# q and k loaded in 32-token blocks and transposed on VectorE, in attention followed by a SoLU feed-forward

## The chip, the cores and the metric

The kernel runs on one core of a Trainium2 chip. The metric is the device time of one execution in microseconds (us). TensorE is called PE in the rows (PEld is its weight load), VectorE DVE, ScalarE ACT, GpSimd POOL; SP is the engine that issues most of the DMA transfers. Each engine works through its own queue of instructions in order, and a wait at the head of a queue holds everything behind it.

## The reference

```python
# q, k, v: (8, 12, 448, 64) float32; rmsnorm is over the 64 elements of a token's row
q_n, k_n = rmsnorm(q, g_q), rmsnorm(k, g_k)
scores = q_n @ k_n.transpose(0, 1, 3, 2) / sqrt(64)
attn = softmax(scores)                     # over keys
x = (attn @ v).transpose(0, 2, 1, 3).reshape(3584, 768)
h = x @ w_in                               # w_in: (768, 1024) float64
solu = h * softmax(h)
out = layernorm(solu) * g_ln @ w_out       # w_out: (1024, 768) float64
```

The weights arrive as 64-bit floats, which the kernel turns into 32-bit ones on the chip.

## The kernel before

The function `fast_path` does all the work; `general_path` is built beside it for large gains and isn't entered here.

**Attention** goes in 48 pairs of heads (8 batches of 6 pairs). In a pair, the 448 tokens lie on 112 partitions as 4 groups (`SP = 112`, `NJ = 4`), token `4p + j` on partition `p` of group `j`. `load` (L477) issues five DMAs on SP's queue: q and k of each head in pieces of 64 elements (256 bytes), and v in pieces of 1 KB. `norm` (L488) squares q and k on ACT (`sq`), sums each row on DVE (L494), and makes the inverse root with Ln and Exp on ACT and a correction step on DVE (L498 to L503). q is scaled by it on POOL (`qn`, L506); k is not scaled: its factor enters later as the scale of the Exp (L537). `qk_transpose` (L513) turns q and k with eight PE transposes of 112x112 into two PSUM tiles (`pt`), which DVE (with the gains, L524) and ACT (L522) copy to `qkT`. `scores` (L526) has four steps `kc`, one for each group of keys: two score matmuls (`s`), two Exps on ACT (`E`), and from the second step on a sum of the Exps on POOL (`es`, L541). `values` (L543) multiplies by v (`o`) and sums the Exps over the keys with a matmul by ones (`sm`), and DVE turns the sums into factors (`r`, `rc`) and writes the result `xT` (L568), at a stride of four elements.

**Weights**: `convert_w` (L450) converts one of 28 pieces: 12 of w_in, whose last product is on POOL (L465), and 16 of w_out, whose last product is on DVE (L468). The tile `tmp` carries it.

**Feed-forward** takes 28 tiles of 128 tokens: `ff_in` (`h`), `ff_solu` (`u`), `ff_transpose` (`pu`, `uT`) and `ff_out` (`po`, `y`).

**The order.** `pair` (L646) lists the pieces of pair n: the score steps, after step 0 the load of pair n+3, after step 1 the values of pair n-1, after step 2 the norm of pair n+2, after step 3 the transposes of pair n+1. Up to four feed-forward pieces go between them; the first may come from pair 12 on, and those of the second half from pair 24 on. The program's order is not the final one: a scheduler orders the instructions of each engine by when it thinks them ready. The buffers bind them too: q and k have 3 buffers, v has 4, `qkT` has 2, and the PSUM tiles `s`, `pt`, `o`, `sm`, `pu` and `po` share 6.

Of the kernel before, what the change touches and what calls it, by code (L numbers as in the profile page):

```python
# [366 lines left out]
def fast_path(  # L367
# [120 lines left out]
    def norm(n):  # L488
        d = st[n]
        sq = work.tile([SP, 2 * NJ * 2, D], FP32, tag="sq", name="sq", bufs=1)  # L490
        nc.scalar.activation(sq, d["qk"].rearrange("p s j h d -> p (s j h) d"), AF.Square)  # L491
        rs = d["rs"] = small.tile([SP, 2, NJ, 2], FP32, tag="rs", name="rs")
        flat = rs.rearrange("p s j h -> p (s j h)")
        nc.vector.tensor_reduce(flat, sq, AX, OP.add)  # L494

        x = small.tile([SP, 4 * NJ], FP32, tag="nx", name="nx")
        y = small.tile([SP, 4 * NJ], FP32, tag="ny", name="ny")
        nc.scalar.activation(y, flat, AF.Ln, scale=1.0 / D, bias=eps[0:SP])  # L498
        nc.vector.tensor_scalar(x, flat, -0.5 / D, -0.5e-6, OP.mult, OP.add)
# [291 lines left out]
```

## Time and profile before

| | |
|---|---|
| median of 3 runs | 1159.03 us (1157.96 to 1160.77) |
| profiled execution | 1159.19 us, of which the span from first to last instruction is 1157.4 us |
| PE busy | 1058.2 us (91% of the span) |
| DVE, ACT, POOL busy | 516.4, 410.9, 394.2 us |
| granted TensorE clock | 0.967 of full speed on average |
| DMA packets | 109047, of them 91056 under 512 bytes |

The shares are averages over stages with different limits. A stage is read from its own window: what is busy in it, at which clock, and which wait ends last. A row of the chain of waits names the work that ended last at each step; a row of a group gives the total busy time and the mean of one instruction in ns.

### The profile page before, as it was taken

The page shows a single profiled execution, that of the slowest core. Times are in us where ns is not written, and L with a number is a line of the kernel's source. Part 1 is how long each engine was busy: PE and PEld are TensorE (multiplying, and loading weights), DVE is VectorE, ACT ScalarE, POOL GpSimd, SP SyncE. Part 2 cuts the span into 40 slices and gives each one's busy share as a digit, 9 for nine tenths or more (in the row PEclk, how much of TensorE's full clock was granted, in tenths as well). Part 3 has the DMA queues.
Part 4 walks back from the last instruction along what each step waited for, and adds up shares of the span by engine and source line. Part 5 has one row for each costly group of instructions (what it writes and reads, how often), then busy time and mean ns, then how long its engine had stood idle before and what let it go on. Part 6 is the DMA issues. An engine that isn't in the chain of part 4 may idle for free.

```text
span 1157.4 us, 10878 instructions
## 1 busy us (share of the span) xinstructions
PE 1058.2 (91%) x3905; PEld 483.1 (42%) x3905; DVE 516.4 (45%) x922; ACT 410.9 (35%) x773; POOL 394.2 (34%) x242
## 2 busy tenths in 40 slices
PE   4666998998768999999999999999999999999997
PEld 2222333342223444444444444444444444455554
DVE  5897446678775333343432334333322333312300
ACT  4554664245555423333323233333322322111111
POOL 4766774245456323233222232232223232100000
PEclk8878999998898999999999999999999999999999
DMA  7421222113332111111111111111111000000001
GB/s 193 143 80 46 63 68 54 52 45 103 89 103 63 48 37 38 38 39 39 38 37 39 38 39 45 24 37 38 46 33 50 23 14 1 14 28 14 14 28 43
DMA packets 109047, 57.50 MB, mean 50 GB/s; under 512 B 91056, under 2 KB 101816, under 8 KB 108984
## 3 DMA queue, kind: packets, MB, share of 16 engines
q1 hardware_dynamic: 104640, 45.63, 15.3%
q10 hardware_dynamic: 4344, 11.08, 2.4%
q8 instruction: 33, 0.54, 0.2%
q14 instruction: 30, 0.25, 0.1%
HBM read 45.68 MB, written 11.01 MB: 49 GB/s over the span
## 4 chain that ended last, share of the span: by engine, by line
PE 73%; DVE 12%; ACT 6%; DMA 4%; issue 3%; POOL 1%; SPq 1%; ACTq 0%; POOLq 0%; DVEq 0%
PE po L630 26%; PE h L587 24%; PE s L533 10%; PE o L553 8%; ACT E L537 2%; PE sm L559 2%; DMA qk<-in_k_dram 2%; PE pt L520 2%; DMA raw<-in_moe_w_out_dram 1%; PE pu L620 1%; DVE tmp L456 1%; DVE rs L494 1%; DVE tmp L463 1%; SPq L485 1%; DVE xT L568 1%
## 5 line engine op out<-in xcount | busy, mean ns | idle before, releaser
L587 PE MATMUL h<-w_in,xT 128*128 128x512 f32 x672 | 310.8, 609 | 17.4 <-DVE xT L568 13.1
L537 ACT ACTIVATE E<-s,rs 112x448 f32<-112x448 f32 x384 | 222.3, 633 | 274.8 <-PE s L533 272.5
L630 PE MATMUL po<-w_out,uT 128*128 128x384 f32 x896 | 301.3, 491 | 5.7 <-ACT uT L621 5.1
L541 POOL TENSOR_TENSOR es<-es,E 112x896 f32<-112x896 f32 x96 | 205.3, 2138 | 257.1 <-ACT E L537 256.3
L533 PE MATMUL s<-qkT 64*112 64x448 f32 x768 | 194.6, 609 | 32.5 <-DVE qkT L524 27.8
L630 PEld LDWEIGHTS po<-w_out,uT 128*128 128x128 f32 x896 | 166.3, 190 | 134.4 <-ACT uT L621 13.2
L587 PEld LDWEIGHTS h<-w_in,xT 128*128 128x128 f32 x672 | 124.1, 193 | 171.6 <-issue 161.0
L541 POOL TENSOR_TENSOR es<-E 112x896 f32<-112x896 f32 x48 | 101.9, 2124 | 244.7 <-ACT E L537 244.4
L553 PE MATMUL o<-E,v 112*64 112x448 f32 x768 | 161.5, 561 | 0.0
L533 PEld LDWEIGHTS s<-qkT 64*112 64x112 f32 x768 | 63.1, 184 | 147.4 <-issue 113.1
L596 DVE TENSOR_REDUCE hmax<-h 128x1 f32<-128x1024 f32 x28 | 34.2, 1222 | 171.3 <-PE h L587 171.3
L631 ACT COPY y<-po 128x384 f32<-128x384 f32 x56 | 26.7, 477 | 225.1 <-PE po L630 225.1
L494 DVE TENSOR_REDUCE rs<-sq 112x16 f32<-112x1024 f32 x48 | 58.4, 1218 | 103.4 <-ACT sq L491 103.1
L553 PEld LDWEIGHTS o<-E,v 112*64 112x64 f32 x768 | 52.6, 141 | 107.6 <-issue 90.1
L563 DVE STREAM_TRANSPOSE r<-sm 128x448 f32<-128x448 f32 x48 | 30.9, 643 | 112.5 <-PE sm L559 112.5
L506 POOL TENSOR_TENSOR qn<-qk,rs 112x512 f32<-112x512 f32 x48 | 53.5, 1115 | 76.5 <-PE pt L520 58.6
L491 ACT ACTIVATE sq<-qk 112x1024 f32<-112x1024 f32 x48 | 50.7, 1057 | 80.5 <-DMA qk<-in_k_dram 80.3
L524 DVE TENSOR_SCALAR qkT<-pt,gcol 128x448 f32<-128x448 f32 x48 | 32.3, 673 | 104.7 <-PE pt L520 104.6
L520 PE MATMUL pt<-ident,qn 112*128 112x112 f32 x192 | 30.4, 284 | 34.0 <-DVE r L563 9.4
L610 POOL TENSOR_TENSOR he<-he,mhalf 128x1 f32<-128x1 f32 x28 | 15.6, 557 | 107.8 <-DVE he L609 107.4
L568 DVE TENSOR_TENSOR xT<-o,r 128x448 f32<-128x448 f32 x48 | 46.4, 970 | 4.9 <-PE h L587 3.7
L520 PEld LDWEIGHTS pt<-ident,qn 112*128 112x128 f32 x192 | 20.0, 147 | 65.2 <-DVE r L563 11.6
(54 smaller groups left out, 676.7 us busy)
## 6 DMA issues: line engine op xcount, KB each, us to landing
qk<-in_q_dram SPq DMA_DIRECT2D x96, 112.0 KB, 3.0
qk<-in_k_dram SPq DMA_DIRECT2D x96, 112.0 KB, 3.0
v<-in_v_dram SPq DMA_DIRECT2D x48, 224.0 KB, 2.7
out_dram<-y ACTq DMA_DIRECT2D x28, 384.0 KB, 2.3
raw<-in_moe_w_in_dram SPq DMA_DIRECT2D x12, 512.0 KB, 5.2
raw<-in_moe_w_out_dram SPq DMA_DIRECT2D x16, 384.0 KB, 3.4
grow<-in_g_q_dram ACTq DMA_DIRECT2D x2, 0.2 KB
grow<-in_g_k_dram ACTq DMA_DIRECT2D x2, 0.2 KB
```

The costliest lines, as they stand in the source:

```text
L491: nc.scalar.activation(sq, d["qk"].rearrange("p s j h d -> p (s j h) d"), AF.Square)
L494: nc.vector.tensor_reduce(flat, sq, AX, OP.add)
L506: nc.gpsimd.tensor_tensor(d["qn"], d["qk"][:, 0].rearrange("p j h d -> p (j h) d"), rs[:, 0].rearrange("p j h -> p (j h) ()").to_broadcast ...
L520: nc.tensor.transpose(pt[:, j * SP : (j + 1) * SP], src, ident[0:SP, 0:SP])
L533: nc.tensor.matmul(s, d["qkT"][hh, 1, kc * SP : (kc + 1) * SP], d["qkT"][hh, 0, :], start=True, stop=True)
L537: nc.scalar.activation(d["E"][:, kc, h], d["s", h], AF.Exp, scale=d["rs"][:, 1, kc, h : h + 1])
L541: nc.gpsimd.tensor_tensor(d["es"], d["E"][:, 0] if kc == 1 else d["es"], d["E"][:, kc], OP.add)
L553: nc.tensor.matmul(o[h * D : (h + 1) * D, :], d["v"][:, h, kc * D : (kc + 1) * D], d["E"][:, kc, h], start=(kc == 0), stop=(kc == NJ - 1),)
L568: nc.vector.tensor_tensor(xTs[b // 2][:, hp, c0 : c0 + S].rearrange("d (p j) -> d j p", j=NJ), o.rearrange("d (j p) -> d j p", j=NJ), r.re ...
L587: nc.tensor.matmul(d["h"][:, hs], xTs[m][:, c, i * P : (i + 1) * P], w_in[:, c, hs], start=(c == 0), stop=(c == KD - 1))
L596: nc.vector.tensor_reduce(nmax, d["h"], AX, OP.max, negate=True)
L630: nc.tensor.matmul(po, d["uT"][:, c], w_out[:, c, hs], start=(c == 0), stop=(c == KF - 1))
```

## The change

- q and k come in 32-token blocks: a partition holds one token of a block for one head and one half of the 64 elements (2 heads x 2 halves x 32 tokens = 128 partitions), and 14 blocks of 32 elements lie side by side. Each of the 8 DMAs writes 32 partitions in pieces of 128 bytes. v comes with token `112 j + p` on partition `p`, in pieces of 256 bytes.
- The squares and sums are over half rows (`part`). A product on PE with a constant matrix `fold` (`ss`, 28 columns) adds the two halves and puts the sum on both partitions. The inverse root is as before, on 28 columns.
- POOL now scales q and k (`qkn`, 128x896), and the Exp has no scale any more.
- One DVE transpose of 32x32 blocks (128x896) makes `qkT`, and ACT multiplies its q half by the gains. The eight PE transposes, `pt` and the two copies are gone.
- With the tokens in order, `xT` is written without a stride.

```diff
+        nc.gpsimd.memset(fold, 0.0)
+        for g in range(4):
+            gs = slice(g * 32, g * 32 + 32)
+            for x in range(2):
+                nc.gpsimd.tensor_copy(fold[gs, g // 2, x], ident[gs, gs])
...
-        d["qk"] = loads.tile([SP, 2, NJ, 2, D], FP32, tag="qk", name="qk", bufs=3)
-        d["v"] = loads.tile([SP, 2, NJ * D], FP32, tag="v", name="v", bufs=4)
+        d["qk"] = loads.tile([P, 2, NB, 32], FP32, tag="qk", name="qk", bufs=3)
+        d["v"] = loads.tile([SP, 2, NJ, D], FP32, tag="v", name="v", bufs=4)
         for s, src in enumerate((q, k)):
-            for h in range(2):
-                nc.sync.dma_start(d["qk"][:, s, :, h], src[b, h0 + h].rearrange("(p j) d -> p j d", j=NJ))
-        nc.sync.dma_start(d["v"], v[b, h0 : h0 + 2].rearrange("h (p j) d -> p h (j d)", j=NJ))
+            for g in range(4):
+                nc.sync.dma_start(
+                    d["qk"][g * 32 : g * 32 + 32, s],
+                    src[b, h0 + g // 2].rearrange("(b t) (x d) -> x t b d", t=32, x=2)[g % 2],
+                )
+        nc.sync.dma_start(d["v"], v[b, h0 : h0 + 2].rearrange("h (j p) d -> p h j d", j=NJ))
...
+        nc.scalar.activation(sq, blocks, AF.Square)
+        nc.vector.tensor_reduce(part, sq, AX, OP.add)
+        ss = ps_t.tile([P, 2 * NB], FP32, tag="t", name="ss")
+        nc.tensor.matmul(ss, fold.rearrange("p h x t -> p (h x t)"), part, start=True, stop=True)
...
+        d["qkn"] = work.tile([P, 2 * NB, 32], FP32, tag="qkn", name="qkn")
         nc.gpsimd.tensor_tensor(
-            d["qn"],
...
+            d["qkn"], blocks, y.rearrange("p b -> p b ()").to_broadcast([P, 2 * NB, 32]), OP.mult
         )
...
-        for s in range(2):
-            pt = ps_t.tile([P, S], FP32, tag="t", name="pt")
-            for j in range(NJ):
...
-                nc.tensor.transpose(pt[:, j * SP : (j + 1) * SP], src, ident[0:SP, 0:SP])
-            if s:
-                nc.scalar.copy(d["qkT"][:, 1], pt)
-            else:
-                nc.vector.tensor_scalar(d["qkT"][:, 0], pt, gcol[:, KF : KF + 1], None, OP.mult)
+        nc.vector.transpose(d["qkT"].rearrange("p s t -> p (s t)"), d["qkn"].rearrange("p b d -> p (b d)"))
+        nc.scalar.activation(d["qkT"][:, 0], d["qkT"][:, 0], AF.Copy, scale=gcol[:, KF : KF + 1])
...
-            nc.scalar.activation(d["E"][:, kc, h], d["s", h], AF.Exp, scale=d["rs"][:, 1, kc, h : h + 1])
+            nc.scalar.activation(d["E"][:, kc, h], d["s", h], AF.Exp)
...
+        nc.vector.tensor_tensor(xTs[b // 2][:, hp, c0 : c0 + S], o, r.rearrange("d b i -> d (b i)"), OP.mult)
```

The scheduler orders the new program anew. Three places show what it makes of it. A number in a name is the serial number of the tile in the program.

PE before, in a pair of the second half, from the third score step (`s_4348`) to the next pair's first (`s_4426`):

```order
L533 MATMUL s_4348<-qkT_4265 112x448
L533 MATMUL s_4350<-qkT_4265 112x448
L587 MATMUL h_4341<-w_in_94,xT_2729 128x512 x6
L533 MATMUL s_4392<-qkT_4265 112x448
L533 MATMUL s_4394<-qkT_4265 112x448
L520 MATMUL pt_4400<-ident_92,qn_4243 128x112 x4
L520 MATMUL pt_4406<-ident_92,qk_4022 128x112 x4
L620 MATMUL pu_4413<-ident_92,u_3711 128x128 x4
L620 MATMUL pu_4419<-ident_92,u_3711 128x128 x4
L533 MATMUL s_4426<-qkT_4399 112x448
```

PE now, the same stretch:

```order
L538 MATMUL s_4220<-qkT_4143 112x448
L538 MATMUL s_4222<-qkT_4143 112x448
L510 MATMUL ss_4231<-part_4228,fold_94 128x28
L586 MATMUL h_4213<-w_in_95,xT_2649 128x512 x6
L538 MATMUL s_4266<-qkT_4143 112x448
L538 MATMUL s_4268<-qkT_4143 112x448
L619 MATMUL pu_4277<-ident_92,u_3605 128x128 x4
L619 MATMUL pu_4283<-ident_92,u_3605 128x128 x4
L538 MATMUL s_4290<-qkT_4273 112x448
```

The two fours of transposes (`pt`) after the fourth score step are gone, and one small product (`ss`) stands after the third.

ACT now, in the same pair (`E_4157`), from its second score step to its third; `sq_4493` belongs to the norm whose product is `ss_4497`, two pairs further on:

```order
L542 ACTIVATE E_4157<-s_4186 112x448
L542 ACTIVATE E_4157<-s_4188 112x448
L507 ACTIVATE sq_4493<-qk_4296 128x896
L542 ACTIVATE E_4157<-s_4220 112x448
L542 ACTIVATE E_4157<-s_4222 112x448
L514 ACTIVATE ny_4234<-ss_4231,eps_100 128x28
L516 ACTIVATE ny_4234<-ny_4234 128x28
```

ACT before, at the start of a pair (`E_4289`); `sq_4494` belongs to the norm that the Ln below it (`ny_4499`) goes on with:

```order
L522 COPY qkT_4265<-pt_4272 128x448
L491 ACTIVATE sq_4494<-qk_4296 112x1024
L631 COPY y_4278<-po_4279 128x384
L537 ACTIVATE E_4289<-s_4290,rs_4100 112x448
L537 ACTIVATE E_4289<-s_4292,rs_4100 112x448
L498 ACTIVATE ny_4499<-rs_4496,eps_99 112x16
```

The square stood four instructions ahead of its own Ln; now it stands two pairs ahead of it.

DVE before, in the third pair, where the weights are converted (`tmp`); each `tmp` number is another piece:

```order
L463 SCALAR_TENSOR_TENSOR tmp_427<-raw_333,tmp_427 128x512
L456 TENSOR_SCALAR tmp_519<-raw_425 128x512
L457 TENSOR_SCALAR tmp_519<-raw_425 128x512
L456 TENSOR_SCALAR tmp_611<-raw_517 128x512
L457 TENSOR_SCALAR tmp_611<-raw_517 128x512
L461 SCALAR_TENSOR_TENSOR tmp_519<-raw_425,tmp_519 128x512
L462 TENSOR_SCALAR tmp_519<-tmp_519 128x512
L463 SCALAR_TENSOR_TENSOR tmp_519<-raw_425,tmp_519 128x512
L461 SCALAR_TENSOR_TENSOR tmp_611<-raw_517,tmp_611 128x512
L456 TENSOR_SCALAR tmp_703<-raw_609 128x512
L494 TENSOR_REDUCE rs_485<-sq_483 112x16
```

DVE now, there, from the values of one pair to the values of the next:

```order
L572 TENSOR_TENSOR xT_289<-o_378,r_390 128x448
L508 TENSOR_REDUCE part_404<-sq_403 128x28
L515 TENSOR_SCALAR nx_409<-ss_407 128x28
L517 TENSOR_TENSOR nx_409<-nx_409,ny_410 128x28
L518 TENSOR_TENSOR nx_409<-nx_409,ny_410 128x28
L464 TENSOR_SCALAR tmp_431<-raw_341 128x512
L519 SCALAR_TENSOR_TENSOR ny_410<-nx_409,ny_410 128x28
L465 TENSOR_SCALAR tmp_431<-raw_341 128x512
L469 SCALAR_TENSOR_TENSOR tmp_431<-raw_341,tmp_431 128x512
L470 TENSOR_SCALAR tmp_431<-tmp_431 128x512
L528 STREAM_TRANSPOSE qkT_514<-qkn_417 128x896
L471 SCALAR_TENSOR_TENSOR tmp_431<-raw_341,tmp_431 128x512
```

The conversions stood two and three in a row ahead of attention's work; now one stands in each pair, among it.

## Rows read from the trace of the kernel before

**Rows 1.** Windows: stretch, length, busy us of PE, PEld, DVE, ACT, POOL; clock, DMA, GB/s.

```profile
0.00:25.00 25.00, 8.66 (x33) 4.77 (x34) 12.37 (x27) 12.93 (x23) 8.56 (x15) 0.95 0.69 173
25.00:173.80 148.80, 115.46 (x508) 45.50 (x508) 104.71 (x178) 84.90 (x158) 104.86 (x58) 0.87 0.31 86
173.80:263.50 89.70, 81.40 (x276) 33.50 (x277) 60.40 (x109) 35.17 (x66) 32.46 (x22) 0.95 0.20 54
263.50:373.60 110.10, 83.86 (x368) 32.37 (x369) 82.83 (x146) 61.39 (x118) 61.72 (x33) 0.89 0.33 86
373.60:1004.00 630.40, 624.40 (x2270) 287.01 (x2270) 227.64 (x413) 198.33 (x374) 183.90 (x113) 1.00 0.13 35
```

**Rows 2.** Timeline of PE: a pair's first scores; start, busy, [idle before].

```profile
25.03 3.33 PE L533 MATMUL s<-qkT 64*112 64x448 f32 x8 [4.29 <-DVE qkT L524]
...
173.76 1.76 PE L533 MATMUL s<-qkT 64*112 64x448 f32 x8 [0.73 <-DVE qkT L524]
...
373.61 1.01 PE L533 MATMUL s<-qkT 64*112 64x448 f32 x4 [0.76 <-DVE qkT L524]
...
734.88 1.01 PE L533 MATMUL s<-qkT 64*112 64x448 f32 x4 [0.97 <-ACT qkT L522]
```

**Rows 3.** Chain of waits between 600 and 740 us: start, us, what.

```profile
650.23 0.94 PE s L533 x4
651.17 0.92 PE pt L520 x8
652.09 5.17 PE h L587 x12
...
667.63 0.75 PE sm L559 x4
668.39 1.02 PE pu L620 x8
```

**Rows 4.** Groups of instructions by form: DVE's work that the change removes or resizes.

```profile
L494 DVE TENSOR_REDUCE rs<-sq 112x16 f32<-112x1024 f32 x48 | 58.4, 1218 | 103.4 <-ACT sq L491 103.1
...
L568 DVE TENSOR_TENSOR xT<-o,r 128x448 f32<-128x448 f32 x48 | 46.4, 970 | 4.9 <-PE h L587 3.7
...
L524 DVE TENSOR_SCALAR qkT<-pt,gcol 128x448 f32<-128x448 f32 x48 | 32.3, 673 | 104.7 <-PE pt L520 104.6
...
L565 DVE STREAM_TRANSPOSE r<-rc 128x448 f32<-128x448 f32 x48 | 30.8, 641 | 0.8
```

**Rows 5.** The same view: ACT and POOL.

```profile
L537 ACT ACTIVATE E<-s,rs 112x448 f32<-112x448 f32 x384 | 222.3, 633 | 274.8 <-PE s L533 272.5 <-POOL es L541 2.1
L541 POOL TENSOR_TENSOR es<-es,E 112x896 f32<-112x896 f32 x96 | 205.3, 2138 | 257.1 <-ACT E L537 256.3 <-POOL w_in L465 0.4
...
L506 POOL TENSOR_TENSOR qn<-qk,rs 112x512 f32<-112x512 f32 x48 | 53.5, 1115 | 76.5 <-PE pt L520 58.6 <-DVE rs L503 17.3 <-DMA qk<-in_k_dram 0.6
L491 ACT ACTIVATE sq<-qk 112x1024 f32<-112x1024 f32 x48 | 50.7, 1057 | 80.5 <-DMA qk<-in_k_dram 80.3
```

**Rows 6.** Timeline of one norm in the PE-bound stretch.

```profile
709.11 1.22 DVE L494 TENSOR_REDUCE rs<-sq 112x16 f32<-112x1024 f32 x1
...
711.49 0.17 DVE L503 SCALAR_TENSOR_TENSOR rs<-nx,ny 112x16 f32<-112x16 f32 x1
```

**Rows 7.** One line's instructions: ns min/median/max of L485's issues on SP.

```profile
L485 SPq DMA_DIRECT2D qk<-in_k_dram x96: 612/621/1485, 2.2 to 894.7; - x96
```

**Rows 8.** DMA issues of the page: KB of one, median us to landing.

```profile
qk<-in_k_dram SPq DMA_DIRECT2D x96, 112.0 KB, 3.0
```

**Rows 9.** Windows again, over one load of q and k alone.

```profile
703.00:709.00 6.00, 6.00 (x22) 3.21 (x20) 3.41 (x9) 2.39 (x5) 5.23 (x4) 1.00 0.34 78
```

**Rows 10.** One line's instructions: ns min/median/max of a small DVE product.

```profile
L501 DVE TENSOR_TENSOR nx<-nx,ny x48: 103/176/1549, 9.9 to 903.9; 112x16 f32<-112x16 f32 x48
```

More of the change, by code (lines that the diff above doesn't have):

```diff
@@ L389, in fast_path @@
     SP = S // NJ
+    NB = S // 32
     NP = H // 2
@@ L396, in fast_path @@
     UB = LAG + 2
-    assert H * D == DM and 2 * D == P and NJ * SP == S and B % 2 == 0 and 2 * S % P == 0
+    assert H * D == DM and 2 * D == P and NJ * SP == S and S % 32 == 0 and B % 2 == 0 and 2 * S % P == 0
     consts = ctx.enter_context(tc.tile_pool(name="consts", bufs=1))
@@ L407, in fast_path @@
     ones = consts.tile([P, D], FP32, name="ones")
+    fold = consts.tile([P, 2, 2, 32], FP32, name="fold")
     w_in = consts.tile([P, KD, DFF], FP32, name="w_in")
@@ L486, in load @@
-        nc.sync.dma_start(d["v"], v[b, h0 : h0 + 2].rearrange("h (p j) d -> p h (j d)", j=NJ))
+            for g in range(4):
[4 more added lines that the diff above has]
+        nc.sync.dma_start(d["v"], v[b, h0 : h0 + 2].rearrange("h (j p) d -> p h j d", j=NJ))
     def norm(n):
         d = st[n]
-        sq = work.tile([SP, 2 * NJ * 2, D], FP32, tag="sq", name="sq", bufs=1)
@@ L491, in norm @@
[L491 to L499, printed above, removed]
+        blocks = d["qk"].rearrange("p s b d -> p (s b) d")
@@ new lines, in norm @@
+        sq = work.tile([P, 2 * NB, 32], FP32, tag="sq", name="sq", bufs=1)
+        part = small.tile([P, 2 * NB], FP32, tag="part", name="part")
+        nc.scalar.activation(sq, blocks, AF.Square)
+        nc.vector.tensor_reduce(part, sq, AX, OP.add)
+        ss = ps_t.tile([P, 2 * NB], FP32, tag="t", name="ss")
+        nc.tensor.matmul(ss, fold.rearrange("p h x t -> p (h x t)"), part, start=True, stop=True)
+        x = small.tile([P, 2 * NB], FP32, tag="nx", name="nx")
+        y = small.tile([P, 2 * NB], FP32, tag="ny", name="ny")
@@ L500, in norm @@
+        nc.scalar.activation(y, ss, AF.Ln, scale=1.0 / D, bias=eps)
+        nc.vector.tensor_scalar(x, ss, -0.5 / D, -0.5e-6, OP.mult, OP.add)
         nc.scalar.activation(y, y, AF.Exp, scale=-0.5)
@@ L502, in norm @@
         nc.vector.tensor_tensor(x, x, y, OP.mult)
-        nc.vector.scalar_tensor_tensor(flat, x, 1.5, y, OP.add, OP.mult)
-        d["qn"] = work.tile([SP, NJ * 2, D], FP32, tag="qn", name="qn")
+        nc.vector.scalar_tensor_tensor(y, x, 1.5, y, OP.add, OP.mult)
+        d["qkn"] = work.tile([P, 2 * NB, 32], FP32, tag="qkn", name="qkn")
         nc.gpsimd.tensor_tensor(
-            d["qn"],
-            d["qk"][:, 0].rearrange("p j h d -> p (j h) d"),
-            rs[:, 0].rearrange("p j h -> p (j h) ()").to_broadcast([SP, NJ * 2, D]),
-            OP.mult,
+            d["qkn"], blocks, y.rearrange("p b -> p b ()").to_broadcast([P, 2 * NB, 32]), OP.mult
         )
@@ L553, in values @@
                 nc.tensor.matmul(
-                    o[h * D : (h + 1) * D, :], d["v"][:, h, kc * D : (kc + 1) * D], d["E"][:, kc, h],
+                    o[h * D : (h + 1) * D, :], d["v"][:, h, kc], d["E"][:, kc, h],
                     start=(kc == 0), stop=(kc == NJ - 1),
```

7 lines of the change are left out of this document (removed).

## Prediction

> **What bounds the kernel now.** I read the table of windows first, because the 40 slices of the page show that PE is not equally busy everywhere. [rows 1] cuts the span where a new regime begins: the start; pairs 1 to 11 (I call it A: 148.8 us, 13.53 per pair); pairs 12 to 15 (B1: 89.7 us, in which feed-forward tiles fill PE); pairs 16 to 23 (B2: 110.1 us, 13.76 per pair); pairs 24 to 47 (C: 630.4 us). The feed-forward tiles after 1004 us hold nothing that the change touches.
>
> In C, PE is busy 624.40 of 630.4 us at full clock; DVE (227.64), ACT and POOL are under 40%. What PE doesn't have to do there is gained nearly in full; what the other engines do more costs nothing as long as it comes in time. All idle time of PE in C is 6.0 us; the largest single wait that I found is the 0.97 us of [rows 2], a pair's first score waiting for ACT's copy of `qkT`, four times, 3.9 us in sum.
>
> In A and B2 no engine is full: in A PE is busy 115.46 of 148.8, DVE 104.71, POOL 104.86, ACT 84.90 [rows 1]. The granted clock is 0.87 there, and [rows 2] shows what that mean hides: pair 1's eight score matmuls take 3.33 us and pair 12's 1.76 us, so that PE falls to its lower level (1.2 GHz) in part of A, after waiting (4.29 us ahead of pair 1). These stages are bound by a loop of waits from engine to engine.
>
> **The change in C.** Taken off PE: eight transposes a pair, one step of 0.92 us in the chain [rows 3]. Added: `ss`, a product with 28 columns. The trace has none of that size. The nearest row is `pu`: eight transposes of 128x128 in 1.02 us, 0.13 each [rows 3]. A product of one such step is the lower end, 0.13; four steps, 0.5, the upper. I take two steps, 0.26. So 24 x (0.92 - 0.26) = **-15.8**. The ends of `ss` give -19.0 to -10.1. The idle 6.0 us may go (to -21.8), but I leave them: the four long waits lie where ACT also has the SoLU's exponential, and with the transposes gone PE only comes earlier to the copy of `uT` behind it.
>
> Two covers make that price valid. First, the fold must not find PE waiting. In the new order of PE `ss` stands between score steps, with a feed-forward piece (5.2 us, [rows 3]) behind it, but the square that feeds it stands two pairs earlier on ACT, so it is long done. Uncovered, PE would stand still for two Exps, the square and the reduce: 1.27 + 0.92 + 1.07 + 0.2 = 3.5 us a pair [rows 4, 5], the square and the reduce scaled by 896/1024. Second, the load must land ahead of that early square, which ACT takes in order, with the Exps behind it. SP now issues eight DMAs of 0.62 us for q and k, then 3.0 us to landing [rows 7, 8]: 8.0 us from the product `qkn` that frees the buffer. Between them PE has two feed-forward pieces and some scores, over 10 us; so it is hidden, with 1 to 5 us to spare.
>
> The other parts lie beside PE in C. DVE per pair: the copy of `qkT` goes (-0.67), the reduce loses an eighth (-0.15), `xT` without its stride lies between 0.64 (a 128x448 transpose) and 0.97 (as now), I take 0.70 (-0.27); the new block transpose of 128x896 costs 1.11 to 1.28, by 0.641 for half of it [rows 4]. Together about +0.1. POOL: `qkn` has 896 elements a row where `qn` had 512 in 1.115 us; scaled that is 1.95, and the `es` product of 896 with two inputs, 2.14, is the upper end [rows 5]. So +0.84 to +1.02 a pair, on an engine that is idle two thirds of C. ACT trades the copy (0.43 to 0.54) for the gain step of the same size, and the square shrinks by an eighth.
>
> **The change in A, B1 and B2.** B1 is PE-bound (81.40 of 89.7): four pairs x 0.66 = **-2.6**.
>
> A and B2 need a new loop. In the new order of A, the square stands in its own pair behind the Exps of step 2, and `qkn` stands on POOL ahead of the last `es`. From one pair's `sm` to the next this is in series: scores 0.94, two Exps 1.27, square 0.92, reduce 1.07, fold 0.26, norm 1.33 (from the reduce's end at 710.33 to 711.66, [rows 6]), `qkn` 1.95, `es` 2.14, `sm` 0.75: 10.6 us, some 10.9 with handing over [rows 3 to 6]. POOL's own work sums to 9.5 now (104.86 / 11) and 10.4 with the longer product; DVE's stays near 9.6, PE's falls from 10.5 to 9.8 [rows 1]. So 10.9 is the floor of the new loop, and 13.53 the present length. The conversions are also spread, one in each pair, where two and three stood ahead of attention's work in DVE's old order; this takes away long waits, but puts five or six DVE instructions into every pair's chain. I take the middle between floor and present, 12.2 us in A. The start: pair 1's scores begin at 25.03 [rows 2]; in the new order they stand behind the fold of the third load. SP has 26 issues of 0.62 us up to that load's last piece, 16.1 us; then 3.0 to land, square 0.92, reduce 1.07, fold 0.26, pair 0's last score step at half clock 1.9, and a good 1 us of handing over: 24.5 (up to 28 if SP or DVE come late). Pair 12 then begins at 24.5 + 11 x 12.2 = 158.7 where it is 173.8: **-15.1**. B2 by the same rule, the middle of 10.9 and 13.76: 12.3, 8 x 1.43 = **-11.7** (the ends: 0 and -22.9).
>
> DMA: one load of q and k has 3584 pieces of 128 bytes where it had 1792 of 256. [rows 9]: a load's 1792 pieces take 0.34 of 16 engines for 6 us, 32.6 engine-us, 18.2 ns a piece. At the same price for a smaller piece the new load takes 65 engine-us, 4.1 us of all 16; v's 896 pieces add 1.0. In a loop of 12 us beside 2.2 us for weights (0.31 x 13.53 less 2.0) that is hidden. The Trainium skill's page "DMA: Bandwidth & Descriptors", section "Specifications", speaks against such pieces: below 512 bytes a transfer falls off the line rate and is read, modified and written. It gives no price; all pieces of q and k were already below that size, and whether 128 bytes cost more than 256 no row here shows (the third rival).
>
> GpSimd's longer product may hold up DVE. [rows 10]: a small DVE product of 0.176 us in the median took 1.549 once. The Trainium skill, "SBUF — State Buffer", section "Terms", says that VectorE and GpSimd share a port pair by a lock held for a whole instruction, the loser blocking fully. The trace agrees by that maximum, if it was such a case. If each of 19 early pairs lost the 0.84 us that the product grows, the sum would be 16 us higher, 1130.
>
> **Sum.** The profiled execution took 1159.19 us, of which 1157.4 are the span; the median of the runs, 1159.03, is the same within 0.02%. -15.1 - 2.6 - 11.7 - 15.8 = -45.2; 1159.2 - 45.2 = **1114.0 us**.
>
> **The rivals.**
> (a) *The early loops gain nothing*: the fold makes PE wait for DVE each pair where the transposes had waited, and the half clock stays. For it: A's waits are on DVE already. Only C and B1 count: 1159.2 - 18.4 = 1140.8.
> (b) *The early loops run at their own length*, 10.9: A then is 24.5 + 11 x 10.9 = 144.4 (-29.4), B2 -22.9, in all -70.7: 1088.5. Against it: POOL would be 95% busy.
> (c) *Small pieces cost double*, 36 ns: q and k take 8.2 us of all 16 engines, v up to 2.0, weights 2.2: 12.4 a pair, some 13 with waits. A: 24.5 + 143 = 167.5 (-6.3), B2 -6.1, in all -30.8: 1128.4.
> (d) *Slower*: the fold stands in PE's queue with the next scores behind it; if the reduce stands behind a DVE conversion, which in turn is held up beside GpSimd's longer products, PE idles, falls to its lower clock, and the pair's matmuls double. At 17 us a pair A takes +37.7 and B2 +25.9, less 18.4: 1204. It decides from 14.6 us a pair on: 11 x (14.6 - 13.53) + 8 x (14.6 - 13.76) = 18.5, what C and B1 gain. The same mechanism in C needs loads that land late, 3.5 us in each of 24 pairs: +84 less the 45.2, also slower. Against it: the order has the square two pairs ahead there.
> (e) *It cancels out*: loops of about 14.6 us, 1159.
>
> **How the numbers follow.** Forecast 0.46, (a) 0.20, (b) 0.11, (c) 0.07, (d) 0.13, (e) 0.03. The range takes in (b) with 8 us for the unknown start and the idle time of C, and (a) with 6 us for a fold of four steps: 1080 to 1147. It leaves out (d), (e) and little more. A measurement of this kernel tells about 0.2%, 2.3 us, from no change: faster 0.84 (forecast, a, b, c), same 0.03, slower 0.13.
>
> **What would show it.** In the profile after: no `pt`; `ss` at about 0.26 us a pair; DVE's block transpose at 1.1 to 1.3; `qkn` at 1.95 to 2.14. PE some 99% busy at full clock in C, with C's length at about 615 us. Pair 12 beginning at about 159 us, pair 24 at about 344. For (a): pair starts where they are now up to 16. For (b): POOL over 90% busy in A. For (c): ACT's square waiting on the DMA of q and k, and a DMA share in A of twice 0.31. For (d): a lower granted clock in A, `ss` or the scores behind it waiting on DVE's reduce, and in C `ss` with a wait of microseconds. The forecast is wrong if C gains under 10 us, or if A's pairs stay above 13.5.

## The result, and the profile after

The changed kernel takes 1133.62 us (median; 1130.65 to 1134.83) where the kernel before took 1158.88 beside it: a ratio of 0.9776, interval 0.9753 to 0.9799. That is 25 us of the 45 that were forecast, within the range.

The table cuts every profiled execution at the first score matmul of pairs 1, 12, 16, 24 and 47, as the prediction did (its A, B1, B2 and C; "rest" begins with pair 47). Times in us; the last two columns are the median of the runs and the ratio to the kernel before with its 95% interval.

| kernel | start | A, 1–11 | B1, 12–15 | B2, 16–23 | C, 24–46 | rest | median | ratio |
|---|---|---|---|---|---|---|---|---|
| before | 25.0 | 148.7 | 89.7 | 110.1 | 602.2 | 181.6 | 1158.9 | 1 |
| forecast | 24.5 | 134.2 | 87.1 | 98.4 | 587.0 | 181.0 | 1114.0 | 0.961 |
| **after** | 28.7 | 136.7 | 83.5 | 107.8 | 595.3 | 180.4 | 1133.6 | 0.978 (0.975–0.980) |
| e1, gain step on VectorE | 28.2 | 135.7 | 87.4 | 111.3 | 593.5 | 180.2 | 1139.4 | 0.983 (0.981–0.985) |
| e2, no sums of Exps | 31.0 | 130.0 | 81.7 | 88.3 | 592.9 | 179.8 | 1103.9 | 0.952 (0.950–0.954) |
| e3, no fold | 31.8 | 205.7 | 90.0 | 104.6 | 598.1 | 180.2 | 1213.9 | 1.047 (1.045–1.049) |
| e4, pieces of 256 B | 30.6 | 136.9 | 83.5 | 107.9 | 595.3 | 180.5 | 1135.9 | 0.979 (0.978–0.981) |
| e5, scaling on VectorE | 29.9 | 131.6 | 84.1 | 109.0 | 594.1 | 180.2 | 1131.1 | 0.976 (0.974–0.977) |
| e6, before + tokens in order | 24.0 | 146.2 | 89.2 | 108.6 | 602.2 | 181.9 | 1149.0 | 0.990 (0.988–0.992) |
| e7, before + k scaled | 27.2 | 151.8 | 88.9 | 113.9 | 599.7 | 181.5 | 1164.3 | 1.003 (1.002–1.005) |
| e8, fold twice | 32.3 | 138.1 | 85.0 | 109.5 | 597.3 | 180.4 | 1144.8 | 0.988 (0.986–0.990) |
| e9, last sum on TensorE | 30.4 | 140.1 | 86.0 | 109.2 | 592.5 | 180.4 | 1137.9 | 0.982 (0.980–0.983) |
| e10, k issued by ScalarE | 30.0 | 138.4 | 85.2 | 105.3 | 593.2 | 180.4 | 1133.7 | 0.978 (0.976–0.980) |
| e11, fold a pair later | 25.3 | 201.5 | 94.9 | 133.3 | 589.6 | 180.3 | 1226.9 | 1.058 (1.056–1.061) |
| e12, fold of a constant | 28.4 | 165.6 | 95.3 | 107.0 | 606.7 | 180.2 | 1185.3 | 1.022 (1.019–1.025) |

The windows of the profile after, cut at the same places (columns as in [rows 1]):

```profile
0.00:28.74 28.74, 8.42 (x24) 4.16 (x26) 9.04 (x25) 9.62 (x19) 9.99 (x23) 0.95 0.75 147
28.74:165.45 136.71, 110.03 (x439) 39.30 (x437) 114.26 (x163) 75.19 (x155) 103.51 (x55) 0.90 0.45 98
165.45:248.99 83.54, 78.89 (x257) 30.74 (x254) 67.89 (x116) 34.87 (x70) 35.03 (x21) 1.00 0.26 53
248.99:356.80 107.81, 88.79 (x331) 31.80 (x329) 88.18 (x141) 53.62 (x115) 68.16 (x33) 0.89 0.40 84
356.80:981.00 624.20, 613.99 (x2133) 276.60 (x2130) 267.12 (x435) 184.43 (x383) 202.04 (x115) 0.99 0.17 36
```

The length of A in the kernel before is the sum of two regimes, which the mean of 13.53 us a pair hides. Cut at the first scores of pair 5, before and after:

```profile
25.03:102.50 77.47, 49.84 (x184) 18.99 (x185) 69.52 (x103) 39.76 (x73) 55.24 (x30) 0.76 0.37 109
102.50:173.76 71.26, 65.58 (x324) 26.44 (x323) 35.15 (x76) 45.14 (x85) 49.55 (x29) 0.99 0.25 62
```

```profile
28.74:76.71 47.97, 38.26 (x160) 13.86 (x158) 39.90 (x57) 27.31 (x56) 36.70 (x20) 0.89 0.47 102
76.71:165.45 88.74, 71.77 (x283) 25.44 (x281) 74.36 (x107) 47.87 (x99) 66.81 (x36) 0.90 0.44 96
```

In the kernel before, all 12 pieces of w_in are converted in pairs 1 to 4, which take 19.4 us each; pairs 5 to 11 take 10.2 each. In the changed kernel one piece is converted in every pair from 1 to 12, and the pairs take 12.0 and 12.7 us each. So the first four pairs gained 29.5 us, and the other seven lost 17.5.

Against [rows 1] VectorE has become busier in every stage from pair 1 on: 114.3 us instead of 104.7 in A, in a shorter stage, and 88.2 instead of 82.8 in B2. The groups by form say why (columns as in [rows 4, 5]):

```profile
L542 ACT ACTIVATE E<-s 112x448 f32<-112x448 f32 x384 | 189.9, 544 | 268.6 <-PE s L538 268.2
L521 POOL TENSOR_TENSOR qkn<-qk,ny 128x896 f32<-128x896 f32 x48 | 83.8, 1746 | 50.9 <-DVE ny L519 31.2 <-DMA qk<-in_k_dram 14.1 <-ACT E L542 3.5
L528 DVE STREAM_TRANSPOSE qkT<-qkn 128x896 f32<-128x896 f32 x48 | 53.0, 1105 | 53.6 <-PE s L538 37.3 <-POOL qkn L521 16.3
L508 DVE TENSOR_REDUCE part<-sq 128x28 f32<-128x896 f32 x48 | 51.7, 1078 | 98.7 <-ACT sq L507 98.5
L507 ACT ACTIVATE sq<-qk 128x896 f32<-128x896 f32 x48 | 45.8, 954 | 3.0 <-DMA qk<-in_k_dram 2.8
L517 DVE TENSOR_TENSOR nx<-nx,ny 128x28 f32<-128x28 f32 x48 | 45.7, 952 | 3.8
L529 ACT ACTIVATE qkT<-qkT,gcol 128x448 f32<-128x448 f32 x48 | 32.3, 672 | 104.4 <-DVE qkT L528 104.4
L572 DVE TENSOR_TENSOR xT<-o,r 128x448 f32<-128x448 f32 x48 | 29.8, 622 | 5.1 <-PE h L586 3.7
L510 PE MATMUL ss<-part,fold 128*128 128x28 f32 x96 | 20.1, 291 | 45.1 <-DVE part L508 45.1
```

The block transpose (1.105 us), the reduce (1.078), `qkn` (1.746) and `xT` (0.622) cost about what was reckoned or less; the gain step on ScalarE (L529) costs 0.672, where 0.43 to 0.54 was reckoned. What stands out is L517, a product of 28 columns: 0.952 us each in the mean. Its counterpart before, L501, had 0.305:

```profile
L501 DVE TENSOR_TENSOR nx<-nx,ny 112x16 f32<-112x16 f32 x48 | 14.6, 305 | 13.6 <-ACT ny L500 13.4
```

In the PE-bound stage the chain of waits shows the fold and the new stall (start, us, what):

```profile
626.27 0.94 PE s L538 x4
627.21 0.34 PE ss L510 x2
627.54 5.25 PE po L629 x16
...
680.53 0.99 PE s L538 x4
681.52 0.53 ACT E L542
682.05 1.09 ACT u L598 x2
683.14 0.43 ACT E L542
683.58 0.18 ACT ny L514
683.75 0.48 ACT uT L620
684.24 0.04 issue
684.28 5.43 PE po L629 x16
```

The fold takes 0.34 us of the chain, against 0.92 for the transposes [rows 3]. The stall of [rows 2] has moved to `po`, which waits for ScalarE's copy of `uT`; TensorE's timeline has it twice in five pairs:

```profile
684.28 5.43 PE L629 MATMUL po<-w_out,uT 128*128 128x384 f32 x16 [0.63 <-ACT uT L620]
716.28 5.43 PE L629 MATMUL po<-w_out,uT 128*128 128x384 f32 x16 [0.67 <-ACT uT L620]
```

In A the waits are these (who waited for whom: us in total, times, longest):

```profile
PE ss L510 <- DVE part L508: 22.4, 10, 3.0
POOL w_in L473 <- DVE tmp L471: 20.2, 11, 2.0
ACT qkT L529 <- DVE qkT L528: 19.1, 6, 3.2
```

TensorE is idle for 26.7 of 136.7 us there, and 22.4 of them stand at the fold: ScalarE's square and VectorE's reduce come right ahead of it in the same pair.

### The profile page after: what moved, and what is told of

The parts are those of the page before. It is cut to its first block, busy times and chain, and to the rows that moved or that the text cites. A ratio compares the mean times of both kernels' runs of the same rounds, so it can differ in the third digit from the quotient of the medians.

```text
span 1132.5 us, 10579 instructions
## 1 busy us (share of the span) xinstructions
PE 1042.8 (92%) x3617; PEld 461.7 (41%) x3617; DVE 573.7 (51%) x922; ACT 375.9 (33%) x773; POOL 420.9 (37%) x251
## 4 chain that ended last, share of the span: by engine, by line
PE 78%; DVE 9%; ACT 6%; DMA 3%; POOL 1%; issue 1%; SPq 1%; ACTq 0%; POOLq 0%; DVEq 0%
PE po L629 26%; PE h L586 24%; PE s L538 12%; PE o L558 11%; PE sm L564 2%; ACT E L542 2%; DVE part L508 2%; DMA raw<-in_moe_w_out_dram 1%; PE pu L619 1%; PE ss L510 1%; ACT sq L507 1%; ACT u L598 1%; POOL es L546 1%; DVE tmp L470 1%; DVE tmp L469 1%
## 5 line engine op out<-in xcount | busy, mean ns | idle before, releaser
L586 PE MATMUL h<-w_in,xT 128*128 128x512 f32 x672 | 304.4, 602 | 7.8 <-DVE u L599 3.6
L542 ACT ACTIVATE E<-s 112x448 f32<-112x448 f32 x384 | 189.9, 544 | 268.6 <-PE s L538 268.2
L538 PE MATMUL s<-qkT 64*112 64x448 f32 x768 | 211.4, 625 | 14.4 <-DVE r L568 8.6
L521 POOL TENSOR_TENSOR qkn<-qk,ny 128x896 f32<-128x896 f32 x48 | 83.8, 1746 | 50.9 <-DVE ny L519 31.2
L508 DVE TENSOR_REDUCE part<-sq 128x28 f32<-128x896 f32 x48 | 51.7, 1078 | 98.7 <-ACT sq L507 98.5
L528 DVE STREAM_TRANSPOSE qkT<-qkn 128x896 f32<-128x896 f32 x48 | 53.0, 1105 | 53.6 <-PE s L538 37.3
L568 DVE STREAM_TRANSPOSE r<-sm 128x448 f32<-128x448 f32 x48 | 30.9, 644 | 84.1 <-PE sm L564 84.1
L529 ACT ACTIVATE qkT<-qkT,gcol 128x448 f32<-128x448 f32 x48 | 32.3, 672 | 104.4 <-DVE qkT L528 104.4
L510 PE MATMUL ss<-part,fold 128*128 128x28 f32 x96 | 20.1, 291 | 45.1 <-DVE part L508 45.1
L564 PE MATMUL sm<-es,ones 112*64 112x448 f32 x192 | 45.5, 544 | 3.6 <-POOL es L546 3.3
L517 DVE TENSOR_TENSOR nx<-nx,ny 128x28 f32<-128x28 f32 x48 | 45.7, 952 | 3.8
```

The costliest lines, as they stand in the source:

```text
L508: nc.vector.tensor_reduce(part, sq, AX, OP.add)
L517: nc.vector.tensor_tensor(x, x, y, OP.mult)
L521: nc.gpsimd.tensor_tensor(d["qkn"], blocks, y.rearrange("p b -> p b ()").to_broadcast([P, 2 * NB, 32]), OP.mult)
L528: nc.vector.transpose(d["qkT"].rearrange("p s t -> p (s t)"), d["qkn"].rearrange("p b d -> p (b d)"))
L538: nc.tensor.matmul(s, d["qkT"][hh, 1, kc * SP : (kc + 1) * SP], d["qkT"][hh, 0, :], start=True, stop=True)
L542: nc.scalar.activation(d["E"][:, kc, h], d["s", h], AF.Exp)
```

## The experiments

**The wait on ScalarE (e1).** ScalarE stands at the gain step until VectorE's transpose is done, with Exps behind it (the third line above).

```diff
-        nc.scalar.activation(d["qkT"][:, 0], d["qkT"][:, 0], AF.Copy, scale=gcol[:, KF : KF + 1])
+        nc.vector.tensor_scalar(d["qkT"][:, 0], d["qkT"][:, 0], gcol[:, KF : KF + 1], None, OP.mult)
```

> The gain step of qkT goes from ScalarE to VectorE, right behind the block transpose. Theory (ScalarE's queue): in the changed kernel ScalarE waits 19.1 us in pairs 1 to 11 and 21.9 us in pairs 16 to 23 for VectorE's block transpose, with Exps queued behind the gain step; with the step on VectorE these waits are gone and the early stages lose 15 to 35 us: 1100 to 1118 us in all. Rival (VectorE is full): VectorE is 84% and 82% busy there and gets 0.3 to 0.7 us more a pair; the early stages stay or lengthen: 1130 to 1145 us. In pairs 24 to 47 both expect at most 2 us of change.

1139.4 us, within the rival's range. A gains 1.0 us, B1 and B2 lose 3.9 and 3.5. The wait on ScalarE was not what holds the early stages. On VectorE the step takes 1.016 us in the mean (L529 of e1), where 0.3 to 0.7 was expected; that this is what B1 and B2 lose by is likely, not shown.

**GpSimd and VectorE (e2, e5, e9).** e2 leaves the sums of the Exps out, e5 moves the scaling, e9 moves the third sum of the early pairs.

```diff
e2
-            nc.gpsimd.tensor_tensor(d["es"], d["E"][:, 0] if kc == 1 else d["es"], d["E"][:, kc], OP.add)
...
-            nc.tensor.matmul(sm[h * D : (h + 1) * D, :], ones[0:SP, :], d["es"][:, h], start=True, stop=True)
+            nc.tensor.matmul(sm[h * D : (h + 1) * D, :], ones[0:SP, :], d["E"][:, 3, h], start=True, stop=True)
e5
-        nc.gpsimd.tensor_tensor(
+        nc.vector.tensor_tensor(
             d["qkn"], blocks, y.rearrange("p b -> p b ()").to_broadcast([P, 2 * NB, 32]), OP.mult
e9
-        if kc:
+        if kc and not (kc == 3 and n < LAST_ON_PE):
...
+            parts = [d["es"][:, h]] + ([d["E"][:, 3, h]] if n < LAST_ON_PE else [])
+            for i, x in enumerate(parts):
```

> The sums of the Exps on GpSimd are left out (the sums over keys take the last group of keys alone), so GpSimd has only the scaling of q and k and the weight products. Theory (VectorE's instructions are stretched beside GpSimd's): the first correction product falls from 0.95 us to 0.2, the steps of the weight conversion from 1.4 to 1.7 us to 0.3 to 0.6, and VectorE's busy time from 574 to under 510 us; pairs 1 to 11 and 16 to 23 fall to 10 to 11 us each, in all 1085 to 1100 us. Rival (VectorE's stretching is off the path): the stages lose only what the last sum costs in the chain, 0 to 1 us a pair: 1115 to 1134 us.

1103.9 us, between the two ranges. The first correction product, one line's instructions (ns min/median/max), after and in e2:

```profile
L517 DVE TENSOR_TENSOR nx<-nx,ny x48: 133/918/2002, 11.0 to 918.3; 128x28 f32<-128x28 f32 x48
```

```profile
L517 DVE TENSOR_TENSOR nx<-nx,ny x48: 131/188/190, 13.3 to 889.1; 128x28 f32<-128x28 f32 x48
```

So this small product is held up by GpSimd's sums: no instruction of the line takes over 0.190 us once the sums are gone. The trace after shows it one by one: all 30 of the 48 that take over 0.2 us begin while a sum runs on GpSimd, and end 0.04 to 0.05 us after it. The Trainium skill, "SBUF — State Buffer", section "Terms", names such a hold: a lock on a port pair that the two engines share, held for a whole instruction. The trace agrees: the longest hold, 2.0 us, is about one sum of 2.1 us. The stages followed less than expected: B2 got 19.5 us shorter, A only 6.7. And e2 takes out two things at once, the hold and the sums in the chain. Its window of B2:

```profile
242.70:330.98 88.28, 80.50 (x331) 30.03 (x329) 67.15 (x143) 53.68 (x117) 13.97 (x8) 0.97 0.50 103
```

> The scaling of q and k goes from GpSimd to VectorE. Theory (in pairs 16 to 23 VectorE is held up beside GpSimd's products, of which this one has grown): GpSimd's busy time falls by 84 us, VectorE's own work grows by 1.2 us a pair (twice the 0.62 us of the 128x448 product), its stretched instructions get shorter; pairs 16 to 23 gain about 1 us each, pairs 1 to 11 nothing: 1122 to 1130 us. Rival (VectorE's own work is the bound): 1.2 us more in each of 19 early pairs: 1150 to 1160 us.

1131.1 us, whose interval overlaps that of the change; both numbers missed, the theory's by 1 us. The stages came out against the theory: A gains 5.1 us and B2 loses 1.2. VectorE is busy 101.5 of its 109.0 us in B2:

```profile
245.63:354.63 109.00, 89.05 (x330) 33.40 (x328) 101.47 (x152) 51.77 (x114) 53.15 (x25) 0.89 0.40 83
```

> The changed kernel, in which pairs 0 to 23 leave the third sum of Exps on GpSimd out and TensorE adds the last group of keys in the sums over keys (four more products, 0.75 us a pair); the result is the same. Theory (the early pairs are held by VectorE's being held up beside GpSimd's sums, and by the last sum in the chain): GpSimd has 2.1 us less a pair; pairs 1 to 11 gain 0.5 to 1 us each, pairs 16 to 23 1 to 2 us, pairs 12 to 15 lose 0.75: 1112 to 1124 us. Rival (TensorE at its lower clock is the bound there): 0 to 1 us more a pair: 1133 to 1150 us.

1137.9 us: the rival's number. In A and B2 GpSimd and VectorE have both become less busy, and both stages are longer:

```profile
30.40:170.46 140.06, 115.61 (x483) 43.47 (x481) 95.81 (x162) 75.77 (x154) 79.20 (x44) 0.90 0.43 95
170.46:256.50 86.04, 82.04 (x273) 32.45 (x271) 64.01 (x117) 35.56 (x72) 28.04 (x18) 1.00 0.26 52
256.50:365.70 109.20, 90.73 (x352) 34.97 (x350) 80.05 (x141) 51.99 (x113) 47.83 (x25) 0.88 0.40 83
```

TensorE's wait at the fold stays (22.9 us in A of e9), and its busy time grows by 5.6 us in A, where the stage grows by 3.3, and by 1.9 in B2, where the stage grows by 1.4. So neither VectorE's nor GpSimd's occupation alone is the bound, and that in e2 it was the hold which made B2 short is not shown.

**The pieces (e4).**

```diff
-                    d["qk"][g * 32 : g * 32 + 32, s],
-                    src[b, h0 + g // 2].rearrange("(b t) (x d) -> x t b d", t=32, x=2)[g % 2],
+                    d["qk"][g * 32 : g * 32 + 32, s].rearrange("t (b x) d -> t b (x d)", x=2),
+                    src[b, h0 + g // 2].rearrange("(x b t) d -> x t b d", t=32, x=2)[g % 2],
```

> q and k are loaded in pieces of 256 bytes, half as many, with the same number of transfers and bytes (a token's two halves then lie side by side, so what is computed is another function of the same size). The order on every compute engine is the same. Theory (the pieces are hidden): the DMA share of pairs 1 to 11 falls from 0.45 towards 0.35, the time stays within 4 us of the changed kernel: 1130 to 1137 us. Rival (small pieces hold up the early loads): pairs 1 to 23 gain 0.5 to 1 us each: 1110 to 1122 us.

1135.9 us, within the theory's range, and every stage from pair 1 on within 0.2 us of the change. The queue rows of the page (packets, MB, share of 16 engines), after and in e4:

```profile
q1 hardware_dynamic: 225984, 45.64, 20.3%
```

```profile
q1 hardware_dynamic: 139968, 45.64, 17.0%
```

86,016 more pieces cost 3.3% of 16 engines over 1132.5 us, 598 us: some 7 ns for each piece more, where a piece of 256 bytes took 18.2 [rows 9]. So two pieces of 128 bytes cost some 25 ns together, 12.6 each, and the time doesn't follow them. The Trainium skill ("DMA: Bandwidth & Descriptors", section "Specifications") asks for at least 512 bytes for the line rate; both sizes lie below that, so no run here compares across it.

**Parts of the change alone (e6, e7).** Both edit the kernel before.

```diff
e6
...
-                nc.sync.dma_start(d["qk"][:, s, :, h], src[b, h0 + h].rearrange("(p j) d -> p j d", j=NJ))
-        nc.sync.dma_start(d["v"], v[b, h0 : h0 + 2].rearrange("h (p j) d -> p h (j d)", j=NJ))
+                nc.sync.dma_start(d["qk"][:, s, :, h], src[b, h0 + h].rearrange("(j p) d -> p j d", j=NJ))
+        nc.sync.dma_start(d["v"], v[b, h0 : h0 + 2].rearrange("h (j p) d -> p h j d", j=NJ))
...
-            xTs[b // 2][:, hp, c0 : c0 + S].rearrange("d (p j) -> d j p", j=NJ),
...
+        nc.vector.tensor_tensor(xTs[b // 2][:, hp, c0 : c0 + S], o, r.rearrange("d b i -> d (b i)"), OP.mult)
e7
+        kk = d["qk"][:, 1].rearrange("p j h d -> p (j h) d")
+        nc.gpsimd.tensor_tensor(
+            kk, kk, rs[:, 1].rearrange("p j h -> p (j h) ()").to_broadcast([SP, NJ * 2, D]), OP.mult
+        )
...
-            nc.scalar.activation(d["E"][:, kc, h], d["s", h], AF.Exp, scale=d["rs"][:, 1, kc, h : h + 1])
+            nc.scalar.activation(d["E"][:, kc, h], d["s", h], AF.Exp)
```

> The kernel before with one part of the change alone: tokens in order on the partitions (v in pieces of 256 bytes), so that xT is written without a stride; the transposes on TensorE stay. Theory (this part pays little): the xT product falls from 0.97 to 0.62 us, 0.35 us a pair on VectorE, of which only the early pairs see something: 1150 to 1159 us. Rival (it was this part that made pairs 12 to 15 faster by more than TensorE's saving): 3 to 4 us there and as much in pairs 16 to 23: 1145 to 1150 us.

1149.0 us, a ratio of 0.990: the rival's number, and two fifths of what the whole change brought. But its stages are not the rival's. Its runs lie between 1145.7 and 1154.0, and the profiled one, at the slow end, shows only 5.3 us of the gain (A 2.5, B2 1.5, the start 1.0, B1 0.5), so where the rest lies is not seen.

> The kernel before with one part of the change alone: k is scaled on GpSimd too (one more product of 512 elements a row, 1.1 us), and the Exp has no scale; transposes on TensorE stay. Theory (GpSimd's longer occupation costs the early pairs): 0.5 to 1 us in each of 19: 1168 to 1178 us. Rival (the Exp without a scale, which fell from 0.633 to 0.544 us in the changed kernel, pays for it: 0.7 us a pair on ScalarE): 1150 to 1160 us.

1164.3 us, 0.3% slower, between the two ranges. A and B2 lose 3.1 and 3.8 us: GpSimd's longer work costs 0.3 to 0.5 us a pair there, less than expected, and C gains 2.5.

**The fold (e8, e3).**

```diff
e8
+        nc.tensor.matmul(ss, fold.rearrange("p h x t -> p (h x t)"), part, start=True, stop=True)
e3
-        ss = ps_t.tile([P, 2 * NB], FP32, tag="t", name="ss")
-        nc.tensor.matmul(ss, fold.rearrange("p h x t -> p (h x t)"), part, start=True, stop=True)
+        ss = part
```

> The changed kernel with the fold made twice. Theory (in pairs 24 to 47 TensorE is the bound, and the fold costs its own time): pairs 24 to 47 take 0.15 to 0.34 us more each, 4 to 8 us, the early pairs 0 to 2 us: 1138 to 1144 us. Rival (the fold is hidden behind other waits): within 2 us of the changed kernel, 1132 to 1136.

1144.8 us, just above the theory's end. In the steady part five pairs take 131.5 us where they took 130.6: 0.18 us for the second fold. C grows by 2.0 us only, the three early stages by 1.4 to 1.7 each, and the start, which varies between versions, by 3.5.

> The product that adds the two halves of a row is left out: the norm goes on with VectorE's half sums. Theory (the fold costs its own time on TensorE, 0.34 us a pair, in the stage of pairs 24 to 47, and 22.4 us of waiting in pairs 1 to 11 that something else would take over): pairs 24 to 47 lose 8 us, the earlier ones 0 to 8: 1118 to 1126 us. Rival (the wait at the fold is what holds the early pairs): pairs 1 to 11 lose 15 to 20 us more: 1100 to 1110 us.

1213.9 us: both failed. Without the fold A takes 205.7 us. C as a whole does not get shorter, though its steady part does: five pairs take 129.5 us instead of 130.6, so that the fold is worth 0.2 us a pair there, as in e8; pair 24 takes 35.2 us instead of 28.2. The scheduler orders the program anew, and TensorE waits elsewhere in A:

```profile
PE s L537 <- ACT qkT L528: 86.5, 10, 10.0
```

The scores now wait for the gain step of their own pair. That made the wait at the fold the question: what if it is taken away with the rest in its place?

**The wait at the fold (e11, e12).** e11 cuts the norm in two and puts the fold behind the values of the next pair; e12 leaves it in place and feeds it a constant.

```diff
e11
...
             if kc == 2 and n + 2 < B * NP:
-                pieces.append(lambda: norm(n + 2))
+                pieces.append(lambda: half_sums(n + 2))
             if kc == 1 and n:
                 pieces.append(lambda: values(n - 1))
+            if kc == 1 and 1 < n + 1 < B * NP:
+                pieces.append(lambda: norm(n + 1))
e12
+        nc.gpsimd.memset(same, 32.0)
...
-        nc.tensor.matmul(ss, fold.rearrange("p h x t -> p (h x t)"), part, start=True, stop=True)
+        nc.tensor.matmul(ss, fold.rearrange("p h x t -> p (h x t)"), same, start=True, stop=True)
```

> The changed kernel with the norm cut in two: squares and half sums of pair n+2 stay behind score step 2 of pair n, the fold and what follows come one pair later, behind the values of the next pair's step 1, so that 3.9 us of other products stand on TensorE between. Theory (in pairs 1 to 11 the wait at the fold, 22.4 of TensorE's 26.7 idle us, is what keeps the early loop long, through the lower clock too): pairs 1 to 11 take 112 to 124 us instead of 136.7, pairs 16 to 23 lose their 4.7 us of that wait: 1108 to 1120 us. Rival (VectorE and GpSimd are late anyway, and the wait moves to the scores, for the block transpose of the next pair): pairs 1 to 11 stay over 130 us: 1126 to 1136 us.

1226.9 us. A pair's first scores in TensorE's timeline of e11:

```profile
101.64 3.33 PE L544 MATMUL s<-qkT 64*112 64x448 f32 x8 [9.67 <-ACT qkT L535]
...
118.51 3.33 PE L544 MATMUL s<-qkT 64*112 64x448 f32 x8 [5.53 <-ACT qkT L535]
```

> The changed kernel, in which the fold multiplies a constant instead of the half sums (squares and half sums are still made, and nothing uses them), so that TensorE never waits at it, while the fold keeps its place behind score step 2 and all that follows it (the scaling, the block transpose, the gain step) stays. Theory (the wait for the half sums, 22.4 us in pairs 1 to 11 and 4.7 us in pairs 16 to 23, with the lower clock that follows it, is what the early stages' gain went into): pairs 1 to 11 take 108 to 122 us instead of 136.7, pairs 16 to 23 some 3 to 8 us less: 1100 to 1116 us. Rival (that wait only stands ahead of the next one, for the chain over GpSimd and VectorE to the next scores): pairs 1 to 11 stay above 128 us: 1124 to 1136 us.

1185.3 us. Its windows of A and B1, and what TensorE waits for in A:

```profile
28.42:194.01 165.59, 104.91 (x428) 36.30 (x428) 108.47 (x163) 73.41 (x153) 99.94 (x54) 0.83 0.35 80
194.01:289.34 95.33, 89.43 (x262) 34.52 (x264) 61.52 (x111) 34.75 (x69) 32.68 (x20) 0.93 0.25 49
```

```profile
PE s L540 <- ACT qkT L531: 60.3, 11, 8.5
```

Both theories fall, and the rivals gave numbers too low. With no wait at the fold the early pairs take 15.1 us (e12) or 18.3 us (e11) instead of 12.4, the granted clock falls to 0.83 and 0.78, and eight scores take 3.33 us in most pairs, as in the kernel before at pair 1 [rows 2]. In e3, e11 and e12 the gain step ends 0.05 us before the scores that read it, in nearly every pair of A; in the changed kernel it ends 5.4 to 7.8 us before. The wait at the fold costs 2 to 3 us in a pair, and in the order that comes with it `qkT` is ready in time. A reason shows in the last correction product, for which GpSimd's scaling waits, one line's instructions in A, after and in e12:

```profile
L519 DVE SCALAR_TENSOR_TENSOR ny<-nx,ny x11: 179/183/189, 28.5 to 152.9; 128x28 f32<-128x28 f32 x11
```

```profile
L521 DVE SCALAR_TENSOR_TENSOR ny<-nx,ny x11: 186/1941/1992, 44.1 to 186.4; 128x28 f32<-128x28 f32 x11
```

After, only the first of the products meets a running sum in A, and GpSimd runs nothing until the others are done; in e12 the last one is held up as well in seven of eleven pairs, by 1.8 us, and the scaling, the transpose and the scores behind it. That this explains the whole of the 29 us is argued, not shown: all three runs have another order of the program too, which no run separates from the wait.

**The start (e10).**

```diff
-                nc.sync.dma_start(
+                (nc.scalar if s and n < 3 else nc.sync).dma_start(
                     d["qk"][g * 32 : g * 32 + 32, s],
```

> The changed kernel, in which ScalarE issues the k transfers of the first three loads. Theory (the start got 3.7 us longer, since SP issues 27 transfers one after the other at 0.52 us): 12 of them leave SP's queue, the start gets back 3 to 6 us: 1127 to 1131 us. Rival (the start waits for the landing of the weight pieces, not for SP): within 2 us, 1132 to 1136 us.

1133.7 us, and a start of 30.0 us: the rival's number, and SP's queue is not what made the start longer. The versions that share this start have 28.2 to 32.3 us, so a microsecond there says nothing. ScalarE's timeline after shows what stands there:

```profile
22.13 0.67 ACT L529 ACTIVATE qkT<-qkT,gcol 128x448 f32<-128x448 f32 x1 [1.45 <-DVE qkT L528]
22.71 1.83 ACT L542 ACTIVATE E<-s 112x448 f32<-112x448 f32 x4
24.41 0.97 ACT L507 ACTIVATE sq<-qk 128x896 f32<-128x896 f32 x1
```

The last line is the square of the third load, which the prediction put at 19.1 us, right behind the landing. SP's issues of that load are done by 15.8 us, near the 16.1 that were reckoned, and the last landing of its q and k on record is at 16.6. But the square comes at 24.4, since it stands in ScalarE's queue behind pair 1's gain step and four Exps. This is read from the timeline; no run moves the square.

No version that computes the same beats the changed kernel beyond the intervals.

## Why the prediction was right, and where its steps failed

The direction and the range held: TensorE is relieved in C, and the early stages gain part of what they could. The gain was 25 us instead of 45, and 1133.6 lies nearer to the numbers of rivals (c), 1128.4, and (a), 1140.8, than to 1114.0. By one of its own signs the forecast is wrong: C was to gain at least 10 us, and gained 6.9, or 8.1 with all that follows. Stage by stage the profiled executions give, forecast against measured: start -0.5 and +3.7; A -14.6 and -12.0; B1 -2.6 and -6.2; B2 -11.7 and -2.3; C with the rest -15.8 and -8.1. The sums are -45.2 and -24.9.

- **A**: the length was right (12.43 us a pair, forecast 12.2), by luck. 13.53 was not the length of a loop but the mean of pairs of 19.4 us with conversions and pairs of 10.2 without, and the middle between it and a chain of 10.9 us was no mechanism. The working saw the conversions spread, and put no number on it: the gain lies in the four pairs that had them, and the pairs that have got one are longer. How much of the 12.0 us is due to the spreading, and how much to the shorter chain, no run separates. What stands in the pair is the wait at the fold, which rival (a) had named, and the chain that would take its place is longer still (e11, e12).
- **B2** is the step that failed: 13.5 us a pair instead of 12.3. The middle between 10.9 and 13.76 was no mechanism here either, and the prediction took VectorE's load as unchanged (+0.1 us a pair). It grew by 5.4 us in eight pairs, since its instructions run longer beside GpSimd's products. The working had this as a side sentence, 0.84 us a pair and 1130 us in all, and did not put it into the sum; that 1130 is near the measured time is luck, since the sentence spreads the loss over A too, which came out 0.2 us a pair above the forecast. The mechanism is only half shown, as e2 takes 21.0 us off VectorE and 19.5 off the stage, but e9 takes 8.1 off VectorE and nothing off the stage. And VectorE is not the only engine that is busier: TensorE's busy time in B2 rose from 83.9 to 88.8 us [rows 1], though the transposes are gone. The scores take 40.4 us of it instead of 33.3, at the same mean clock of 0.89, and the feed-forward products that stand in the stage 11.4 instead of 8.6. Why the scores take longer, and which of the two engines sets the length, stays open.
- **C**: the place was right, the size half. The fold cost 0.34 us, not 0.26 (bounds 0.13 and 0.5). Five pairs in the steady part went from 133.0 to 130.6 us, 0.48 a pair instead of 0.66: 0.92 - 0.34 = 0.58, less the idle time, which rose from 0.97 to 1.30 in five pairs, and a small rest. "I leave them" on the idle time was the slip: the working says that TensorE comes earlier to the copy of `uT`, and puts that at nothing. In all of C the idle time rose from 6.0 to 10.2 us, and 3.6 of them stand in pair 24, where TensorE waits for VectorE. That pair takes 28.2 us instead of 22.1, at a granted clock of 0.82 instead of 1.00, and pairs 24 to 28 take 126.6 instead of 125.1. In the changed kernel VectorE still converts two pieces of w_out in it; the kernel before had none after pair 22.

```profile
356.80:385.00 28.20, 24.62 (x84) 12.06 (x82) 19.83 (x35) 11.02 (x22) 10.46 (x6) 0.82 0.30 55
```

```profile
368.75 2.05 PE L586 MATMUL h<-w_in,xT 128*128 128x512 f32 x2 [3.58 <-DVE u L599]
```

- The two covers held: in C no wait at the fold, and the square never waits for its load long (3.0 us in all pairs, where the kernel before had 80.3, [rows 5]).
- **B1** gained 3.6 us more than forecast. TensorE's busy time fell by 2.5 us, as reckoned; its idle time fell from 8.3 to 4.7 and its clock rose from 0.95 to 1.00, and both had been taken as given.
- **The start** got 3.7 us longer instead of 0.5 shorter: the sum had the third load's square right behind its landing, at 19.1 us, and it came at 24.4, behind other work on ScalarE (e10).
- **Rival (a)** is right on the wait at the fold, and nearly on B2, which gained 2.3 us, but A gained 12.0. **Rival (c)** falls (e4); the DMA share of A is 0.45, not twice 0.31. **Rival (d)** has not come, but its price is real: e3 and e11 run A at 18 to 19 us a pair, and are 5 and 6% slower than the kernel before. It came by the scores waiting for the gain step, not by the scores behind the fold.
